# Turns given to the DMA queue by the slot that needs them, and the last keys' scores turned by DMA

## The chip, the cores and the metric

The kernel runs on one core of a Trainium2 chip. The metric is the device time of one execution in microseconds. Its engines are TensorE (PE in the profile; PEld is its weight load), VectorE (DVE), ScalarE (ACT), GpSimd (POOL) and SyncE (SP), which in this kernel issues every DMA, one after the other, from one list.

## What is computed

Two layers, one behind the other, for 8 batches of 3136 rows:

```python
scores = (1 / S) * z @ z.T           # z: 3136 x 64, S = 3136
attn   = maximum(scores, 0) ** 2
x      = u * (attn @ v)              # u, v: 3136 x 256
h      = xT @ U @ V                  # U: 3136 x 32, V: 32 x 3136, over the rows
u2     = x + hT
out    = u2 + maximum(u2 @ w_ch1, 0) @ w_ch2     # 256 -> 1024 -> 256
```

The matrix of scores is symmetric: the scores of keys J against queries g are the transpose of the scores of keys g against queries J. The kernel uses this, and so does the change.

## The kernel before, in words

**Tiles and groups.** The 3136 rows of a batch are 24 tiles of 128 and a rest of 64. Four tiles are a group of 512 rows, so a batch has six full groups (0 to 5) and a short one (6) with the last 64 rows. The program goes through 56 slots, one for each (batch, group), written (b, g) here; `t` counts them and `NG` is 7. In slot (b, g) the attention of group g of batch b is accumulated (`av_stream`, closed by `av_end`), and work of other stages lies between: scores for later slots, the low-rank part (`t1_all`, `u2_unit`) one batch behind, and the two channel products (`ch1_part`, `ch2_stream`) of the item one batch and one slot behind. The short slot (b, 6) has `av_small` in place of the attention stream.

**Scores and turns.** A block holds the squared scores of 512 keys J against 512 queries g, in bf16; there are 20 buffers for blocks. `score_pairs` makes half a block with two matmuls into one PSUM buffer of two banks, `rectify` (ScalarE, L335, or VectorE, L331) evicts it with the relu, and `square` (VectorE, L325) squares it. Only blocks with J >= g are made by matmuls, save for some of batch 0 that are made twice. The others are turned: a transposing DMA (`issue_turn`, L351) writes block (g, J) from block (J, g), 512 KB each, 15 in a batch (fewer in batch 0).

**The last 64 keys.** They meet the queries in two ways. For the last 64 queries, `score_small` makes one tile `attn_small` (128 keys, 25 tiles, 64 queries), which `av_small` reads in the short slot; before the change it is called in slot (b, 5). For the queries of groups 0 to 5, a job named "last", one for two groups, makes the scores of the last 64 keys against 2 x 512 queries: two matmuls side by side on the two halves of the rows, an eviction and a square into the tile `last_sb` (two buffers). `av_end` (L609) reads it as the last step of the attention of a group. `jobs_of` (L924) adds such a job for groups 0, 2 and 4 of each batch, and the jobs of group g are made in the slot before it; those of group 0 are spread over three slots of the batch before, and its last job falls into the short slot (for batch 1: into slot (1, 0)).

**The order of the work.** It is written out ahead of time by a planner that keeps a clock in units of 256 matmul columns (`clock`, `pe`) and an estimate of when ScalarE, VectorE and the DMA queue are free (`free_at`, `book`, `queued`). PSUM has four buffers (`take_ps` takes the one that it believes free first), one of them held by the attention stream. `emit` places the units of the other stages at given places between the attention's matmuls, later if it believes too few PSUM buffers free. `run_held` runs what is due, then issues turns: those whose source is squared wait in `ready_turns`, and one goes to SP whenever the estimate says that the queue is free and no `urgent` transpose is pending. It takes them in the order of the slot's group J, then the batch, then g. If the attention stream comes to a block that has not been issued, it issues the turn at that point (L521).

**Other DMAs on SP, in the same list.** Loads of u (L286), v (L234) and z (L211, L205), each batch's z transposed as a whole (`z_turn_dma`, L297, in slot (b, 2) for batch b + 1), the transpose of x into `u2T` for ch1 (`x_turn`, L634), and the stores of the result (L849). In slot (b, 0) the loads of z for the next batch come first, and u2T's transpose follows when `u2_unit` and its cast are done.

Of the kernel before, what the change touches and what calls it, by code (L numbers as in the profile page):

```python
# [18 lines left out]
def kernel(  # L19
# [79 lines left out]
    unturned = {}  # L99
    ready_turns = []  # L100
    urgent = []

    def book(eng, ready, cost):
        free_at[eng] = max(free_at[eng], ready) + cost
        return free_at[eng]

    def queued(kb, turned=False):

        book("sp", clock[0], kb * (17 / 256 if turned else 15 / 512))

    def hold(due, f):
        held.append((due, len(held), f))

    def run_held(now=None):
        now = clock[0] if now is None else now
        while True:
            ripe = [h for h in held if h[0] <= now]
            if not ripe:
                break
            h = min(ripe, key=lambda e: (e[0], e[1]))  # L120
            held.remove(h)
            h[2]()
        while ready_turns and free_at["sp"] <= now and not urgent:
            issue_turn(min(ready_turns, key=lambda e: (e[0], e[2], e[1])))

    def pe(cost):
        clock[0] += cost
# [218 lines left out]
    def issue_turn(e):  # L346
        ready_turns.remove(e)
        J, g, b = e
        src = blocks[b, g, J]
        blocks[b, J, g] = take_block()  # L350
        nc.sync.dma_start_transpose(  # L351
            out=blocks[b, J, g][1].rearrange("p j (q c) -> p (j q) c", c=P),
            in_=src[1].rearrange("p j c -> p (j c)"),
        )
        book("sp", clock[0], 34)
        if unturned.pop(src[0]):
            free_blocks.append(src[0])

    def score_pairs(jobs):

        made = []
        for b, g, job in jobs:
            zzT = zzTs[b]
            k, ps = take_ps()
            if job == "last":
                keys, cols = [NF, NF], [groups[g + jj][0] for jj in range(2)]
            else:
                J, h = job
                keys, cols = [J * GT + 2 * h + jj for jj in range(2)], [groups[g][0]] * 2
            pair(  # L370
                k,
                [
                    (
                        jj,
                        jj,
                        dict(
                            out=ps[:, jj, :],
                            lhsT=half(zzT, jj, keys[jj] * P, P),
                            rhs=half(zzT, jj, cols[jj], GW),
                            start=True,  # L380
                            stop=True,
                        ),
                    )
                    for jj in range(2)
                ],
                GW,
            )
            if job == "last":
                lasts[b, g // 2] = pool.tile([P, 2, GW], BF16, name="last_sb")
                made.append((lasts[b, g // 2], k, ps, None, None))  # L390
                continue
            if h == 0:
                blocks[b, g, J] = take_block()
            made.append(
                (
                    blocks[b, g, J][1][:, 2 * h : 2 * h + 2, :],
                    k,
                    ps,
                    (J, g, b) if h == 1 and J > g and not made_twice(b, J, g) else None,
                    (b, g, J),  # L400
                )
            )
        return made
# [19 lines left out]
        score_finish(score_pairs(jobs))  # L423


    def score_small(b, g):
        zzT = zzTs[b]
        g0, gw = groups[g]
        per = GW // gw
        att = pool.tile([P, NT, gw], BF16, name="attn_small")  # L430
        smalls[b] = att
        made = []
        npair = NF // 2
        for p0 in range(0, npair, per):
            n = min(per, npair - p0)
            pk, ps = take_ps()
            for k in range(n):
                pair(
                    pk,
                    [  # L440
                        (
                            jj,
                            jj,
                            dict(
                                out=ps[:, jj, k * gw : (k + 1) * gw],
                                lhsT=half(zzT, jj, (2 * (p0 + k) + jj) * P, P),
                                rhs=half(zzT, jj, g0, gw),
                                start=(k == 0),
                                stop=(k == n - 1 and (jj == 1 or p0 + n < npair)),
                            ),  # L450
                        )
                        for jj in range(2)
                    ],
                    gw,
                )
            made.append((p0, n, pk, ps))
        corner = ps[:, 0, n * gw : (n + 1) * gw]
        nc.tensor.matmul(
            out=corner,
            lhsT=half(zzT, 0, NF * P, P),  # L460
            rhs=half(zzT, 0, g0, gw),
            start=False,
            stop=True,
        )
        for p0, n, k, pp in made:
            dst = att[:, 2 * p0 : 2 * (p0 + n), :].rearrange("p (k j) c -> p j k c", j=2)
            src = pp[:, :, : n * gw].rearrange("p j (k c) -> p j k c", c=gw)
            for jj in range(2):
                nc.scalar.activation(out=dst[:, jj], in_=src[:, jj], func=AF.Relu, scale=scale)
                ps_free[k] = book("act", clock[0] + 3, 5)  # L470
        nc.scalar.activation(out=att[:TAIL, NF, :], in_=corner[:TAIL], func=AF.Relu, scale=scale)
        nc.vector.memset(att[TAIL:, NF, :], 0.0)
        ps_free[pk] = book("act", clock[0] + 3, 2.5)
        hold(ps_free[pk], lambda: square(att, 9))
# [87 lines left out]
    def av_small(b, g):  # L562
        k, ps = take_ps()
        rows = groups[g][1]
        xs[b, g] = pool.tile([P, GT, D], BF16, name="x_bf", bufs=8)
        for jt in range(NT):
            c = jt % 2
            for h in range(2):
                nc.tensor.matmul(  # L569
                    out=ps[c * hp : c * hp + rows, h, :D],  # L570
                    lhsT=smalls[b][h * hp : (h + 1) * hp, jt, :],
                    rhs=v_bfs[b][h * hp : (h + 1) * hp, jt, :],
                    start=(jt < 2),
                    stop=(jt >= NT - 2),
                    tile_position=(h * hp, c * hp),
                )
        pe(NT / 2 + 2)
        u1 = u_sbs[b, g]
        four_sums(k, ps, u1[:rows, 1:3, :])
        nc.vector.tensor_tensor(  # L580
            out=xs[b, g][:rows, 0, :], in0=u1[:rows, 1, :], in1=u1[:rows, 0, :], op=ALU.mult
        )
        book("dve", clock[0] + 3, 3)
# [24 lines left out]

    def av_end(b, g, box):  # L609

        last = lasts[b, g // 2]
        for a in range(2):
            pair(
                box["k"],
                crossed(
                    0,
                    a,
                    lambda h, q: dict(
                        out=four(box["ps"])[:, q, :],
                        lhsT=last[h, g % 2, q * P : (q + 1) * P],  # L620
                        rhs=v_bfs[b][h, NF, :],
                        start=False,
                        stop=(a == 1),
                    ),
                ),
                D,
            )
        av_out(b, g, box)
# [295 lines left out]
    def jobs_of(b, g):  # L924
        js = [J for J in range(NQ) if J >= g or made_twice(b, g, J)]
        j = [(b, g, (J, h)) for J in js for h in range(2)]
        if g % 2 == 0:
            j.append((b, g, "last"))
        return j

# [153 lines left out]
    for b in range(B):  # L1084
        for g in range(NQ):
# [7 lines left out]
                todo[t + 1] += new[12:] if b == 1 else []  # L1093
            elif b == 0 and g == 0:
                todo[0] += new[4:]
            else:
                todo[t] += new

# [3 lines left out]

    direct = (B - 1, 0)
    for t in range(n_items):
        att = items[t]
        u2i = items[t - NG] if t >= NG else None
        mix = items[t - NG - 1] if t > NG else None
# [26 lines left out]
                hold(clock[0] + 5 + 22 * i, lambda f=f: load(f))  # L1134
        if t <= NG:
            hold(clock[0] + 60, lambda t=t: load_u(*items[t + 1]))
        if b_next < B and g_now == 2:
            while spare:
                spare.pop(0)()
            z_turn_dma(b_next)  # L1140
# [14 lines left out]
        one = lambda h, way: lambda: ch1_part(*mix, h, way, box1)  # L1155
        hs = list(range(0, NH, 2)) if mix else []
        full = mix and mix[1] < NQ
        if av and g_now == NQ - 1:
            qm.append((55, 2, False, lambda: score_small(att[0], NQ)))
        if av and full:  # L1160

            last = nA - 9
# [111 lines left out]
```

## Time and profile before

| what | us |
|---|---|
| median of 3 runs (1003.33 to 1005.26) | 1004.55 |
| the profiled execution | 1002.76 |
| its span | 1001.0 |
| TensorE busy | 984.9 (98%) |
| VectorE busy | 655.9 (66%) |
| ScalarE busy | 520.3 (52%) |
| DMA queue, packets' share of 16 engines' span | 77.1% |

How to read it: times are microseconds from the start of the span; an engine is busy when one of its instructions runs. Matmuls overlap, so what one of them costs is seen from the start of one to the start of the next, not from its length. In a timeline, a row is a run of equal instructions: start, length until the last one ends, engine, line of the kernel, operation, output <- inputs with buffer numbers left out, shape, count, and in brackets the idle time before it with what ended it. Rows of one engine overlap by the length of the last instruction. SP's rows are the times in which it issues a DMA; the transfer lands later. L169 is a helper that issues all paired matmuls, so these are told apart by their tiles: `zzT` alone is scores, `v_bf,blk` attention, `u2T,w_bf` ch1, `w_bf,blk` ch2, `t_sb,V_bf` the u2 product, `v_bf,last_sb` av_end. Batch 0 differs from the others (loads of the weights, blocks made twice); from batch 1 on the program nearly repeats by batch.

### The profile page before, as it was taken

Reading aid. Unit: us, or ns where it says so; the run is one execution under the profiler, and the core shown is the slowest. Engines: PE = TensorE matmul, PEld = TensorE weight load, DVE = VectorE, ACT = ScalarE, POOL = GpSimd, SP = SyncE. Lnnn points to the kernel's source line nnn. Section 1 sums busy time; section 2 is a strip of 40 time slices with the busy share of each in tenths; the row PEclk is TensorE's granted clock in tenths of the full one; section 3 lists DMA queues with packets and bytes.
Section 4 is the critical chain, followed back from the end, with each engine's and each line's share of the span. In section 5 each row is a group of like instructions: output and inputs, shape, how many; then the busy total and the mean of one; then the engine's idle time right before and its main releaser. Section 6 shows DMA issues by size and latency. Waiting matters only on the chain.

```text
span 1001.0 us, 35345 instructions
## 1 busy us (share of the span) xinstructions
PE 984.9 (98%) x16179; PEld 820.1 (82%) x16179; DVE 655.9 (66%) x822; ACT 520.3 (52%) x597; POOL 16.6 (2%) x24
## 2 busy tenths in 40 slices
PE   6999999999999999999999999999999999999997
PEld 4898888877888788887888878888888877787776
DVE  6986856668566776666856677566775667653453
ACT  6896843457335473345643465435653356522453
POOL 4100000000000000000000000000000000000000
PEclk9999999999999999999999999999999999999999
DMA  8997898978886799877897789976889586863142
GB/s 260 197 252 177 188 182 182 196 164 190 168 205 137 177 174 183 191 129 183 157 217 166 141 179 176 198 170 139 182 186 194 142 170 143 154 126 89 45 104 95
DMA packets 337061, 167.84 MB, mean 168 GB/s; under 512 B 312336, under 2 KB 315408, under 8 KB 336912
## 3 DMA queue, kind: packets, MB, share of 16 engines
q1 hardware_dynamic: 336912, 165.59, 77.1%
q8 instruction: 126, 2.06, 0.9%
q14 instruction: 23, 0.19, 0.1%
HBM read 62.56 MB, written 25.69 MB: 88 GB/s over the span
## 4 chain that ended last, share of the span: by engine, by line
PE 94%; DVE 3%; ACT 2%; issue 0%; DMA 0%; POOLq 0%; ACTq 0%
PE ps L169 92%; DVE blk L325 1%; PE ps L569 1%; ACT blk L810 1%; PE ps L646 1%; DVE out_sb L719 1%; ACT blk L335 1%; PE ps L861 0%; DMA blk<-in_z_dram 0%; DVE blk L331 0%; DVE blk L847 0%; DVE blk L1065 0%; DVE x_bf L602 0%; PE ps L306 0%; ACT zzT L315 0%
## 5 line engine op out<-in xcount | busy, mean ns | idle before, releaser
L169 PEld LDWEIGHTS <-blk 64*128 64x128 bf16 x12288 | 647.6, 94 | 123.6 <-POOLq L159 8.7
L169 PE MATMUL ps<-v_bf,blk 64*128 64x256 bf16 x9216 | 620.4, 269 | 3.3 <-DVE blk L325 2.8
L335 ACT ACTIVATE blk<-ps 128x1024 bf16<-128x1024 f32 x334 | 333.1, 1027 | 330.3 <-PE ps L169 328.5
L325 DVE TENSOR_TENSOR blk<-blk 128x1024 bf16<-128x1024 bf16 x352 | 237.3, 700 | 34.1 <-ACT blk L335 33.3
L169 PE MATMUL ps<-u2T,w_bf 64*128 64x512 bf16 (+1 forms) x1792 | 240.7, 349 | 0.7
L807 DVE TENSOR_SCALAR blk<-ps 128x1024 bf16<-128x1024 f32 (+1 forms) x114 | 132.1, 1159 | 96.1 <-PE ps L169 95.2
L169 PE MATMUL ps<-w_bf,blk 64*128 64x256 bf16 x3072 | 194.1, 269 | 0.2
L169 PE MATMUL ps<-zzT 64*128 64x512 bf16 (+1 forms) x944 | 144.9, 341 | 2.3 <-ACT zzT L315 1.7
L810 ACT ACTIVATE blk<-ps 128x1024 bf16<-128x1024 f32 (+1 forms) x110 | 93.4, 859 | 82.7 <-PE ps L169 75.2
L169 PEld LDWEIGHTS <-w_bf 64*128 64x128 bf16 x1792 | 95.8, 94 | 27.4 <-POOLq L159 3.0
L602 DVE TENSOR_TENSOR x_bf<-ps,u_sb 128x1024 bf16<-128x1024 f32 x48 | 58.7, 1222 | 62.0 <-PE ps L169 61.9
L719 DVE TENSOR_TENSOR out_sb<-ps,x_bf 128x1024 f32<-128x1024 f32 (+1 forms) x49 | 54.2, 1107 | 51.1 <-PE ps L169 50.8
L847 DVE TENSOR_TENSOR out_sb<-ps,out_sb 128x1024 f32<-128x1024 f32 x42 | 51.3, 1222 | 18.3 <-PE ps L169 18.3
L169 PEld LDWEIGHTS <-zzT 64*128 64x128 bf16 x944 | 46.1, 95 | 8.4 <-issue 2.6
L335 ACT ACTIVATE last_sb<-ps 128x1024 bf16<-128x1024 f32 x23 | 23.6, 1024 | 28.4 <-PE ps L169 28.4
L169 PE MATMUL ps<-t_sb,V_bf 64*128 64x256 bf16 x200 | 21.1, 269 | 0.0
L331 DVE TENSOR_SCALAR blk<-ps 128x1024 bf16<-128x1024 f32 x14 | 17.1, 1224 | 5.6 <-PE ps L169 4.8
L191 DVE CAST v_bf<-stage 128x1024 bf16<-128x1024 f32 (+1 forms) x30 | 20.0, 670 | 0.0
L191 DVE CAST x_bf<-out_sb 128x1024 bf16<-128x1024 f32 x28 | 19.3, 690 | 0.5
L169 PE MATMUL ps<-v_bf,last_sb 64*128 64x256 bf16 x192 | 18.8, 269 | 0.0
L847 DVE TENSOR_TENSOR blk<-ps,blk 128x1024 f32<-128x1024 f32 x6 | 7.3, 1225 | 16.0 <-PE ps L169 15.9
L588 ACT COPY u_sb<-ps 64x512 f32<-64x512 f32 x8 | 4.7, 582 | 23.9 <-PE ps L569 23.9
(68 smaller groups left out, 255.7 us busy)
## 6 DMA issues: line engine op xcount, KB each, us to landing
u_sb<-in_u_dram SPq DMA_DIRECT2D x48, 512.0 KB, 5.1
stage<-in_v_dram SPq DMA_DIRECT2D x42, 512.0 KB, 6.0
out_dram<-out_sb SPq DMA_DIRECT2D x42, 512.0 KB, 3.1
stage<-in_z_dram SPq DMA_DIRECT2D x7, 512.0 KB, 5.4
blk<-in_v_dram SPq DMA_DIRECT2D x6, 512.0 KB, 6.2
out_dram<-blk SPq DMA_DIRECT2D x6, 512.0 KB, 2.6
blk<-in_moe_w_ch_dram SPq DMA_DIRECT2D x4, 512.0 KB, 4.9
stage<-in_z_dram SPq DMA_DIRECT2D x7, 256.0 KB, 5.7
```

The lines of the kernel that those rows point to most:

```text
L169: ins = nc.tensor.matmul(**args)
L191: nc.vector.tensor_copy(out=out, in_=in_)
L325: nc.vector.tensor_tensor(out=a, in0=a, in1=a, op=ALU.mult)
L331: nc.vector.tensor_scalar(out=dst, in0=src, scalar1=scale, scalar2=0.0, op0=ALU.mult, op1=ALU.max)
L335: nc.scalar.activation(out=dst, in_=src, func=AF.Relu, scale=scale)
L569: nc.tensor.matmul(out=ps[c * hp : c * hp + rows, h, :D], lhsT=smalls[b][h * hp : (h + 1) * hp, jt, :], rhs=v_bfs[b][h * hp : (h + 1) * hp ...
L602: nc.vector.tensor_tensor(out=xs[b, g][:rows, :n, :], in0=four(box["ps"])[:rows, :n, :], in1=u_sbs[b, g][:rows, :n, :], op=ALU.mult,)
L646: nc.tensor.matmul(out=pt[c * R : (c + 1) * R, 0, :D], lhsT=U_bf[:rows, it, :], rhs=xs[b, g][:rows, q, :], start=(it < NREP), stop=(it + N ...
L719: nc.vector.tensor_tensor(out=o[:rows, :n, :], in0=four(ps)[:rows, :n, :], in1=x, op=ALU.add)
L807: nc.vector.tensor_single_scalar(out=r, in_=ps[:, :, :gw], scalar=0.0, op=ALU.max)
L810: nc.scalar.activation(out=r, in_=ps[:, :, :gw], func=AF.Relu)
L847: nc.vector.tensor_tensor(out=o, in0=acc, in1=o, op=ALU.add)
```

## The change

**Turns.** They are now taken by `needed`: the slot that reads the block (batch times 7 plus J), then g. A turn goes to SP when the estimate of the queue is free, or up to 30 units ahead of that when it is needed in this slot or the next. The estimate counts less for each transfer: 30 in place of 34 for a turned block, 15/256 in place of 17/256 a KB for other transposes, 12/512 in place of 15/512 for plain ones.

**Last keys.** For batches 1 to 7 the "last" jobs are gone. At the start of slot (b, 0), `last_turn` gives SP one transpose of 24 tiles of `attn_small` (128 x 1536 bf16) into a tile `last_sb` of 128 x 12 x 128, behind the loads of that slot; `av_end` reads that tile. For this, `score_small` of batch b is called one batch earlier, in slot (b - 1, 5), and that of batch 0 in slot (0, 4). It makes the key tiles in the order 0, 2, 1, 3 of each four (`place_of`), so that the two halves of the rows of the turned tile hold the query tiles that `av_end` pairs; `av_small` reads them in that order too. Batch 0 keeps its three last jobs, which now use the first part of the same single buffer; those for groups 2 and 4 are made one slot later, in the slot that reads them.

```diff
@@ queued, run_held, issue_turn
+    slot = [0]
+    def needed(e):
+        J, g, b = e
+        return b * NG + J, g
...
-        book("sp", clock[0], kb * (17 / 256 if turned else 15 / 512))
+        book("sp", clock[0], kb * (15 / 256 if turned else 12 / 512))
...
-        while ready_turns and free_at["sp"] <= now and not urgent:
-            issue_turn(min(ready_turns, key=lambda e: (e[0], e[2], e[1])))
+        while ready_turns and not urgent:
+            e = min(ready_turns, key=needed)
+            if free_at["sp"] > now + (30 if needed(e)[0] <= slot[0] + 1 else 0):
+                break
+            issue_turn(e)
...
-        book("sp", clock[0], 34)
+        book("sp", clock[0], 30)
@@ score_pairs
-                lasts[b, g // 2] = pool.tile([P, 2, GW], BF16, name="last_sb")
+                flat = last_tile().rearrange("p n c -> p (n c)")
+                lasts[b, g // 2] = flat[:, : 2 * GW].rearrange("p (a c) -> p a c", c=GW)
@@ new, ahead of score_small
+    def place_of(jt):
+        if jt == NF:
+            return jt
+        return jt // GT * GT + (0, 2, 1, 3)[jt % GT]
+    def last_tile():
+        return pool.tile([P, NF // 2, P], BF16, name="last_sb", bufs=1)
+    def last_turn(b):
+        lasts[b] = last_tile()
+        nc.sync.dma_start_transpose(
+            out=lasts[b], in_=smalls[b][:, :NF, :].rearrange("p t c -> p (t c)")
+        )
+        book("sp", clock[0], 26)
@@ score_small
-                                lhsT=half(zzT, jj, (2 * (p0 + k) + jj) * P, P),
+                                lhsT=half(zzT, jj, place_of(2 * (p0 + k) + jj) * P, P),
@@ av_small
-                    lhsT=smalls[b][h * hp : (h + 1) * hp, jt, :],
+                    lhsT=smalls[b][h * hp : (h + 1) * hp, place_of(jt), :],
@@ av_end
-        last = lasts[b, g // 2]
+        def last(h, q):
+            if b:
+                return lasts[b][h, 2 * g + q % 2, :]
+            return lasts[b, g // 2][h, g % 2, q * P : (q + 1) * P]
...
-                        lhsT=last[h, g % 2, q * P : (q + 1) * P],
+                        lhsT=last(h, q),
@@ jobs_of
-        if g % 2 == 0:
+        if g % 2 == 0 and b == 0:
             j.append((b, g, "last"))
@@ the jobs of each slot
+            elif b == 0 and g and g % 2 == 0:
+                todo[t] += new[:-1]
+                todo[t + 1] += new[-1:]
@@ the loop over slots
+        slot[0] = t
...
+        if g_now == 0 and t:
+            last_turn(att[0])
...
-        if av and g_now == NQ - 1:
-            qm.append((55, 2, False, lambda: score_small(att[0], NQ)))
+        if av and t == NQ - 2:
+            qm.append((55, 2, False, lambda: score_small(0, NQ)))
+        if av and g_now == NQ - 1 and b_next < B:
+            qm.append((55, 2, False, lambda: score_small(b_next, NQ)))
```

## The prediction

> **What bounds the kernel now.** I read the busy shares first, then the chain of waits, then the groups by form, and at last the timelines of the few places where TensorE stops.
>
> The page, busy time and chain:
> ```profile
> span 1001.0 us, 35345 instructions
> ...
> PE 984.9 (98%) x16179; PEld 820.1 (82%) x16179; DVE 655.9 (66%) x822; ACT 520.3 (52%) x597; POOL 16.6 (2%) x24
> ...
> PE 94%; DVE 3%; ACT 2%; issue 0%; DMA 0%; POOLq 0%; ACTq 0%
> ```
> TensorE is busy from end to end, and the granted clock is 1.0 throughout. The waits name no DMA on TensorE at all: no turn ever came late. So only two things shorten the time: fewer matmul columns, and less of the small idle time in front of matmuls. The groups that the change thins out, by form:
> ```profile
> L169 PE MATMUL ps<-zzT 64*128 64x512 bf16 x752 | 140.7, 380 | 2.3 <-ACT zzT L315 1.7
> ...
> L335 ACT ACTIVATE last_sb<-ps 128x1024 bf16<-128x1024 f32 x23 | 23.6, 1024 | 28.4 <-PE ps L169 28.4
> ...
> L325 DVE TENSOR_TENSOR last_sb<-last_sb 128x1024 bf16<-128x1024 bf16 x24 | 16.4, 683 | 0.2 <-ACT last_sb L335 0.2
> ```
> The "last" job is made 24 times: two 512-column matmuls, one eviction of 1024 ns, one square of 683 ns. The mean of 380 ns is the length of one matmul, and they overlap; what one costs TensorE is read from starts. TensorE's timeline in the short slot (group 6) of batch 2:
> ```profile
> 331.42 0.60 PE L169 MATMUL ps<-u2T,w_bf 64*128 64x512 bf16 x4
> 331.85 0.39 PE L169 MATMUL ps<-zzT 64*128 64x512 bf16 x2
> 332.07 1.90 PE L169 MATMUL ps<-u2T,w_bf 64*128 64x512 bf16 x16
> 333.79 0.39 PE L169 MATMUL ps<-zzT 64*128 64x512 bf16 x2
> 334.27 1.47 PE L169 MATMUL ps<-u2T,w_bf 64*128 64x512 bf16 x12
> ```
> Eight pairs run from 332.07 to 333.79: 0.215 us a pair. The pair at 333.79 is a "last" job, and the next starts 0.48 us later, so 0.27 us of that is a stall. ScalarE in the same stretch says for what:
> ```profile
> 333.20 1.02 ACT L810 ACTIVATE blk<-ps 128x1024 bf16<-128x1024 f32 x1
> 334.22 1.02 ACT L335 ACTIVATE last_sb<-ps 128x1024 bf16<-128x1024 f32 x1
> ```
> The matmul at 334.27 needs the PSUM buffer that the eviction of 333.20 gives back at 334.22. The "last" job took the buffer before it (given back at 333.30).
>
> The second stop is in slot (b, 1); TensorE, then VectorE:
> ```profile
> 364.18 0.60 PE L169 MATMUL ps<-v_bf,blk 64*128 64x256 bf16 x8
> 364.61 0.38 PE L169 MATMUL ps<-zzT 64*128 64x512 bf16 x2
> 364.83 0.71 PE L169 MATMUL ps<-v_bf,blk 64*128 64x256 bf16 x10
> 365.66 0.39 PE L169 MATMUL ps<-zzT 64*128 64x512 bf16 x2
> ```
> ```profile
> 364.38 1.23 DVE L719 TENSOR_TENSOR out_sb<-ps,x_bf 128x1024 f32<-128x1024 f32 x1
> ```
> Five pairs from 364.83 need 5 x 0.109 = 0.55 us (0.109 from 8 matmuls in 0.43), yet the score pair starts 0.83 us later, when L719 has emptied its buffer: a stall of 0.28 us. Both stops come back every 121.92 us, the period of a batch in the chain (332.28, 454.20, 576.11).
>
> **The change, part by part.**
>
> *Last jobs.* Batches 1 to 7 lose three each: 21 pairs x 0.2157 = 4.53 us of TensorE, with no cover since TensorE is the bound. The 21 evictions (21 x 1.02 us of ScalarE) and 21 squares lie beside it. av_end keeps its matmuls and reads another tile.
>
> *Short slot, batches 1 to 6.* The last job left the short slot, so the matmul after it takes the buffer that is free at 333.30, while TensorE gets there at 333.79: the 0.27 us goes. 6 x 0.27 = 1.6 us. What is late next is the last relu before ch2 (ended 337.01, cost 0.10 us by a gap before 337.06); it may eat some, so 1.0 to 2.2, and I take 1.6.
>
> *Slot (b, 1).* With one job fewer, the list of places spreads: in the built program the score after u2 now stands behind 6 attention pairs and no other score, and the buffer that it takes is not the one which L719 empties. The stop shows in batches 2 to 6, at 243.75, 365.66, 487.58, 609.49 and 731.41. Between none and all, 0 to 5 x 0.28 = 1.4; I take two thirds, 0.9, since evictions near it shift too.
>
> *Slot (1, 0).* At 109.43 TensorE waits for the cast of v_bf, the end of a DVE queue without a gap from 101.40, in which the square of last_sb (0.69 us at 102.01) goes. The stall there is 0.64 us. Bounds 0 and 0.64; I take 0.3, as that queue is also reordered.
>
> *score_small one batch earlier.* The same 8 calls; 0.35 us of TensorE each (the 12 pairs run from 321.57 to 321.92), moved from group 5 of batch 7 to group 4 of batch 0. Evictions and square (16 x 0.61, 16 x 0.42 and 8 x 0.99 us in all) go along, onto engines at 52% and 66%. Zero, between -0.3 and +0.5.
>
> *The new transpose, 7 times.* 128 x 1536 bf16 = 393 KB on the only queue. It goes to SP behind the loads of z at the start of slot (b, 0). Its place in SP's list:
> ```profile
> 346.03 1.55 SPq L205 DMA_DIRECT2D stage<-in_v_dram  x2
> 350.30 2.21 SPq L634 DMA_TRANSPOSE u2T<-x_bf  x1
> ```
> SP is free from 347.58 to 350.30. A block's turn of 512 KB holds SP 2.83 us (median of line 351), u2T's of 256 KB 1.25, so this one some 2.0: it fits the gap. The DMA engines, by windows (the last two numbers are share and GB/s):
> ```profile
> 343.50:348.50 5.00, 5.00 (x102) 4.23 (x98) 4.48 (x8) 3.03 (x6) 0.00 (x0) 1.00 1.00 338
> 349.50:351.50 2.00, 2.00 (x44) 1.78 (x37) 1.66 (x5) 1.24 (x3) 0.00 (x0) 1.00 0.10 25
> 354.00:356.00 2.00, 2.00 (x38) 1.60 (x34) 1.93 (x5) 0.69 (x1) 0.00 (x0) 1.00 1.15 214
> ```
> They stand idle from 349.5 to 351.5, and turns move 214 GB/s, so 393 KB take 1.84 us: about the size of that hole. Landing by the rows (3.3 us for u2T, 5.2 for a block) is some 4.2 us after issue, 351.8; av_end reads at 356.02. Behind it waits u2T's turn, issued 350.30, landed 354.7, first read 356.68: margin 2.0 us. If the transpose is pushed out of the hole by up to 1.84 us, u2T still lands by 356.5. Bounds 0 and 7 x 1.0; I take 0.5 in all. The Trainium skill, page "Advanced Engine Details and Errata", section "X-Bar Transpose (TRN2)", says that transposing DMAs run as fast as plain ones; here they run at 214 GB/s against 338 for loads, so the measurement decides. By the page it would be 1.16 us instead of 1.84, more margin, and the sum the same.
>
> *Order and figures of the turns.* Turned blocks stand, in the built programs, at least 22 us of matmuls ahead of their first reader before and 27 us after, against 5 us to land: neither gain nor loss from their order. What moves is queue order. In slot (b, 2) one more block's turn (2.83 us on SP) now stands between the turn of zzT and that of u2T; u2T landed at 390.05 there and is read at 395.93, 5.9 us of margin. The blocks that ScalarE writes into have, in the built program, been read for the last time 3.7 us or more before. Zero, between -0.2 and +2.
>
> *Batch 0.* Its three last tiles now share one buffer, and two of the jobs move one slot on; ScalarE's write waits for the av_end before, while TensorE goes on. Zero.
>
> Sum: -4.53 - 1.6 - 0.9 - 0.3 + 0.5 = -6.8 us. The profiled execution took 1002.76 us (span 1001.0 and 1.76 around it), which becomes 996.0; it lies 1.8 below the median of the runs, 1004.55, which becomes 997.7.
>
> **The rivals.**
>
> *Columns alone.* The stops move instead of going (a later eviction or the cast is late). Then -4.5 and up to +1.5 of new waits: 1000.0 to 1001.5. Against it: the chain is empty elsewhere.
>
> *Slower: u2T late at the start of slot (b, 1).* The new transpose misses the hole, and SP's 2.0 us and the engines' 1.84 both delay u2T: 3.84 less the margin of 2.0 is a stall of 1.84 in each of 7 batches, +12.9; net +6.1, 1010.6. It decides from 2.0 + 6.8 / 7 = 3.0 us of delay. For it: in batch 4 the margin was 1.15 us (landed 477.44, read 478.60). Against it: idle DMA engines just there. The Trainium skill, "DMA: Bandwidth & Descriptors", section "Queues, rings and completion order", has each engine consume its ring in order, which is the mechanism of this rival; no row here shows a u2T packet behind another transpose's in that slot.
>
> *Nothing gained: the saving goes into half-late u2T turns.* A delay near 3.0 us in each batch gives about 1004.5.
>
> **How the numbers follow.** Forecast 0.62, columns alone 0.22, nothing gained 0.07, slower 0.09. 0.2% (2 us) is about what a measurement here can tell. All of the gains taken whole, -4.53 - 2.2 - 1.4 - 0.64 = -8.8, give 995.8, and runs spread by 1.2 below the median: low 994.5. Columns alone with new waits reach 1001.5, with spread 1002.2: high. Outside lie the two last cases and a little of the first. Faster 0.84, same 0.07, slower 0.09.
>
> **What would show it.** Right: 42 matmuls and 21 evictions fewer; no gap before the ch1 matmuls of the short slot; the period 121.92 down to about 120.9; the wait for L719 gone or small; the new transpose landed before 353; no DMA in TensorE's waits. Wrong: TensorE waiting for u2T or last_sb at the start of slot (b, 1), or new waits on evictions where scores moved.

## The result, and the profile after

The changed kernel takes 998.55 us (median of 6 runs, 997.68 to 999.23) against 1004.36 (6 runs, 1003.33 to 1005.26): a ratio of 0.9946, with a 95% interval of 0.9936 to 0.9956. The forecast was 997.7 us and a gain of 6.8; the gain is 5.8. The profiled execution took 997.68 us, its span is 995.9.

The page of the changed kernel, busy times and chain (line numbers have moved: L178 was L169, L344 L335, L334 L325, L750 L719, L198 L189, L596 L569):
```profile
span 995.9 us, 35255 instructions
...
PE 979.2 (98%) x16137; PEld 781.5 (78%) x16137; DVE 635.6 (64%) x793; ACT 506.4 (51%) x584; POOL 16.8 (2%) x24
...
PE 97%; DVE 1%; ACT 1%; DMA 1%; issue 0%; POOL 0%; SPq 0%; POOLq 0%
```
42 matmuls are gone, and TensorE's share of the chain went from 94% to 97%: VectorE and ScalarE are hardly in it any more. The groups by form:
```profile
L178 PE MATMUL ps<-zzT 64*128 64x512 bf16 x710 | 131.2, 381 | 1.7 <-ACT zzT L324 1.7
...
L334 DVE TENSOR_TENSOR last_sb<-last_sb 128x1024 bf16<-128x1024 bf16 x3 | 2.1, 687 | 0.2 <-ACT last_sb L344 0.2
L344 ACT ACTIVATE last_sb<-ps 128x1024 bf16<-128x1024 f32 x2 | 2.0, 1021 | 0.6 <-PE ps L178 0.6
```
752 became 710, and three squares are left, those of batch 0. The chain in order of time shows the length of a batch by the 50 matmuls of the short slot, first before and then after:
```profile
337.67 1.54 PE ps L569 x50
...
459.59 1.54 PE ps L569 x50
```
```profile
338.10 1.54 PE ps L596 x50
...
458.83 1.54 PE ps L596 x50
```
A batch takes 120.73 us, where it took 121.92. The 1.19 us are three pairs (0.65), the stop in the short slot (0.27) and the one in slot (b, 1) (0.28), to the rounding. TensorE in the short slot of batch 2, timeline:
```profile
332.30 0.62 PE L178 MATMUL ps<-u2T,w_bf 64*128 64x512 bf16 x4
332.73 0.40 PE L178 MATMUL ps<-zzT 64*128 64x512 bf16 x2
332.95 3.21 PE L178 MATMUL ps<-u2T,w_bf 64*128 64x512 bf16 x28
335.97 0.27 PE L178 MATMUL ps<-w_bf,blk 64*128 64x256 bf16 x1
```
The 14 pairs of ch1 run from 332.95 to 335.97 in one row: 0.216 each, no stop. In slot (b, 1):
```profile
364.38 0.38 PE L178 MATMUL ps<-t_sb,V_bf 64*128 64x256 bf16 x4
364.60 0.82 PE L178 MATMUL ps<-v_bf,blk 64*128 64x256 bf16 x12
365.26 0.38 PE L178 MATMUL ps<-zzT 64*128 64x512 bf16 x2
365.47 0.59 PE L178 MATMUL ps<-u2T,w_bf 64*128 64x512 bf16 x4
```
Six attention pairs take 0.66 us and the score pair follows at once.

One wait grew. TensorE and VectorE in slot (1, 0) before:
```profile
108.04 0.93 PE L169 MATMUL ps<-v_bf,blk 64*128 64x256 bf16 x14
109.43 0.83 PE L169 MATMUL ps<-v_bf,blk 64*128 64x256 bf16 x12 [0.46 <-DVE v_bf L191]
```
```profile
108.69 0.68 DVE L191 CAST v_bf<-stage 128x1024 bf16<-128x1024 f32 x1
```
TensorE and ScalarE there after:
```profile
108.81 1.36 PE L178 MATMUL ps<-v_bf,blk 64*128 64x256 bf16 x22
111.94 1.05 PE L178 MATMUL ps<-v_bf,blk 64*128 64x256 bf16 x16 [1.77 <-ACT v_bf L198]
```
```profile
106.18 2.92 ACT L344 ACTIVATE blk<-ps 128x1024 bf16<-128x1024 f32 x3 [0.74 <-PE ps L178]
108.99 1.05 ACT L198 CAST w_bf<-blk 128x1024 bf16<-128x1024 f32 x1
109.92 1.04 ACT L344 ACTIVATE blk<-ps 128x1024 bf16<-128x1024 f32 x1
110.84 1.05 ACT L198 CAST v_bf<-stage 128x1024 bf16<-128x1024 f32 x1
```
The cast of v_bf, which VectorE did before, is now on ScalarE behind another cast and an eviction. From start to start, TensorE comes to 111.94 1.95 us later than the matmuls before it need; before the change it lost 0.64 us there, at 109.43.

The new transpose in SP's timeline at the start of slot (2, 0):
```profile
225.70 1.24 SPq L214 DMA_DIRECT2D stage<-in_v_dram  x2
227.04 2.25 SPq L448 DMA_TRANSPOSE last_sb<-attn_small  x1
229.96 1.64 SPq L665 DMA_TRANSPOSE u2T<-x_bf  x1
```
It sits in SP's gap, and SP is done with it (229.29) before u2T's turn goes out. No DMA appears in TensorE's waits.

Not all of the difference of the two traces belongs to the change. Up to 30 us the lists of all engines are the same, and yet one and the same matmul of slot (0, 2) starts here:
```profile
32.24 0.28 PE L169 MATMUL ps<-v_bf,blk 64*128 64x256 bf16 x2 [0.94 <-DVE blk L325]
```
```profile
33.27 0.28 PE L178 MATMUL ps<-v_bf,blk 64*128 64x256 bf16 x2 [0.93 <-DVE blk L334]
```
before in the first fence, after in the second. Over the profiles of this study, that matmul starts at 32.0 to 33.8 us. So the difference of the spans, 5.1 us, holds 1.0 us of a slower beginning, and without it is 6.1. The last section compares all runs from this matmul on.

### The profile page after: what moved, and what is told of

Its sections match the earlier page's. It is cut to its first block, busy times and chain, and to the rows that moved or that the text cites. A ratio compares the mean times of both kernels' runs of the same rounds, so it can differ in the third digit from the quotient of the medians.

```text
span 995.9 us, 35255 instructions
## 1 busy us (share of the span) xinstructions
PE 979.2 (98%) x16137; PEld 781.5 (78%) x16137; DVE 635.6 (64%) x793; ACT 506.4 (51%) x584; POOL 16.8 (2%) x24
## 4 chain that ended last, share of the span: by engine, by line
PE 97%; DVE 1%; ACT 1%; DMA 1%; issue 0%; POOL 0%; SPq 0%; POOLq 0%
PE ps L178 94%; PE ps L596 1%; PE ps L677 1%; DVE blk L334 1%; DMA blk<-in_v_dram 1%; PE ps L892 0%; ACT blk L344 0%; ACT blk L841 0%; DVE blk L340 0%; POOL z_bf L229 0%; DVE blk L878 0%; DVE x_bf L629 0%; POOL v_bf L249 0%; PE ps L315 0%; ACT v_bf L198 0%
## 5 line engine op out<-in xcount | busy, mean ns | idle before, releaser
L178 PEld LDWEIGHTS <-blk 64*128 64x128 bf16 x12288 | 616.1, 94 | 154.3 <-POOLq L168 8.8
L178 PE MATMUL ps<-v_bf,blk 64*128 64x256 bf16 x9216 | 614.0, 270 | 3.2 <-ACT v_bf L198 1.8
L344 ACT ACTIVATE blk<-ps 128x1024 bf16<-128x1024 f32 x334 | 334.3, 1027 | 363.3 <-PE ps L178 361.5
L334 DVE TENSOR_TENSOR blk<-blk 128x1024 bf16<-128x1024 bf16 x352 | 237.4, 699 | 33.6 <-ACT blk L344 33.1
L178 PE MATMUL ps<-u2T,w_bf 64*128 64x512 bf16 (+1 forms) x1792 | 237.2, 349 | 0.2
L178 PE MATMUL ps<-w_bf,blk 64*128 64x256 bf16 x3072 | 193.8, 269 | 0.2
L838 DVE TENSOR_SCALAR blk<-ps 128x1024 bf16<-128x1024 f32 (+1 forms) x111 | 128.4, 1156 | 96.5 <-PE ps L178 95.6
L178 PE MATMUL ps<-zzT 64*128 64x512 bf16 (+1 forms) x902 | 135.3, 341 | 1.7 <-ACT zzT L324 1.7
L178 PEld LDWEIGHTS <-w_bf 64*128 64x128 bf16 x1792 | 91.9, 94 | 28.9 <-POOLq L168 4.1
L750 DVE TENSOR_TENSOR out_sb<-ps,x_bf 128x1024 f32<-128x1024 f32 (+1 forms) x49 | 54.2, 1106 | 50.3 <-PE ps L178 49.9
L178 PEld LDWEIGHTS <-zzT 64*128 64x128 bf16 x902 | 41.8, 95 | 7.4 <-ACT zzT L324 2.2
L178 PE MATMUL ps<-t_sb,V_bf 64*128 64x256 bf16 x200 | 20.8, 269 | 0.0
L200 DVE CAST v_bf<-stage 128x1024 bf16<-128x1024 f32 x28 | 19.1, 683 | 0.0
L178 PE MATMUL ps<-v_bf,last_sb 64*128 64x256 bf16 x192 | 18.6, 269 | 0.0
L198 ACT CAST v_bf<-stage 128x1024 bf16<-128x1024 f32 (+1 forms) x20 | 17.1, 856 | 0.0
L617 DVE TENSOR_TENSOR u_sb<-ps,u_sb 64x512 f32<-64x512 f32 x8 | 5.5, 683 | 17.1 <-ACT u_sb L615 17.1
```

Source lines behind the costliest of these rows:

```text
L178: ins = nc.tensor.matmul(**args)
L198: nc.scalar.copy(out=out, in_=in_)
L200: nc.vector.tensor_copy(out=out, in_=in_)
L334: nc.vector.tensor_tensor(out=a, in0=a, in1=a, op=ALU.mult)
L344: nc.scalar.activation(out=dst, in_=src, func=AF.Relu, scale=scale)
L750: nc.vector.tensor_tensor(out=o[:rows, :n, :], in0=four(ps)[:rows, :n, :], in1=x, op=ALU.add)
```

## The experiments

Each ran beside the kernel before on the same chip, four on one chip and four on another; ratios are against that kernel.

**The turn rule alone.** The kernel before with `needed`, the gate and the smaller figures, without anything of the last keys:

```diff
-            issue_turn(min(ready_turns, key=lambda e: (e[0], e[2], e[1])))
+            e = min(ready_turns, key=needed)
+            if free_at["sp"] > now + (30 if needed(e)[0] <= slot[0] + 1 else 0):
+                break
+            issue_turn(e)
...
+ (and 30, 15 / 256, 12 / 512 for 34, 17 / 256, 15 / 512)
```

> The kernel before with the new rule and figures for the turns alone; the last jobs stay. TensorE, ScalarE and VectorE have the same lists as before; SP's list alone changes. Theory A (the gain is 21 score pairs and two kinds of PSUM stops, the turns' order does nothing, since every turned block is issued 27 us or more ahead of its reader): 1004.4, within 1 us, TensorE's waits unchanged, the stops of 0.28 and 0.27 us still there in each batch. Theory B (part of the 5.8 us comes from the turn rule, which lets blocks or u2T land earlier): 1 to 3 us faster. Theory C (the rule costs, and hides more gain of the last jobs): 1 to 3 us slower, a TensorE wait on a DMA.

Measured: 1003.36 us against 1003.49, ratio 0.9997 (0.9987 to 1.0007). Theory A: all stops of 0.27 and 0.28 us are where they were, and no DMA is waited for. On the kernel before, the rule is worth nothing that can be measured.

**The last keys alone.** The changed kernel with the old rule and the old figures. The lists of TensorE, VectorE and ScalarE are those of the changed kernel.

```diff
-            e = min(ready_turns, key=needed)
-            if free_at["sp"] > now + (30 if needed(e)[0] <= slot[0] + 1 else 0):
-                break
-            issue_turn(e)
+            issue_turn(min(ready_turns, key=lambda e: (e[0], e[2], e[1])))
...
- (and 34, 17 / 256, 15 / 512 again)
```

> The changed kernel with the old rule and the old figures for the turns. Theory A: the same as the changed kernel, 998.5, within 1 us, and the wait of 2 us in slot (1, 0) still there, since VectorE and ScalarE have the same lists. Theory B: 1 to 3 us of the gain is lost, 999.5 to 1001.5. Theory C: 1 to 3 us faster than the changed kernel.

Measured: 1004.99 us, ratio 1.0019 (1.0009 to 1.0028). No theory had this: the whole gain is gone, and the run is a little slower than the kernel before. TensorE's timeline and then SP's say where:
```profile
203.97 0.28 PE L175 MATMUL ps<-v_bf,blk 64*128 64x256 bf16 x2
210.25 1.25 PE L175 MATMUL ps<-v_bf,blk 64*128 64x256 bf16 x10 [6.00 <-DMA blk<-blk]
```
```profile
197.72 6.11 SPq L357 DMA_TRANSPOSE blk<-blk  x2
203.93 1.88 SPq L662 DMA_TRANSPOSE u2T<-x_bf  x1
205.86 2.06 SPq L357 DMA_TRANSPOSE blk<-blk  x1
```
The last turned block that slot (1, 5) reads is issued at 205.86, when TensorE has already come to it, and lands 4.3 us later. In the built program this turn stands directly ahead of its reader; every other turn stands at least 13 us of matmuls ahead. Three turns of batch 2, which are read 46 to 73 us after their place, were taken ahead of it: the old order compares the group first and the batch second, so groups 1, 2 and 3 of batch 2 pass group 5 of batch 1. On the kernel before, the same order never let a turn fall under 12.8 us. With the new transpose booked on the estimate (26 units), the queue counts as free later, the turn waits longer, and the attention stream itself has to call for it (L521 in the kernel before). Built without that booking, the program issues this turn 11.8 us of matmuls ahead of its reader; that program was not run, so the booking's part is read from the programs and not shown by a time. (The two expectations that follow put the turn 1.9 us ahead of its reader and 18 us or more in the other programs; counted by start-to-start costs, the distances are these smaller ones, and the turns ahead of it are three and not two.) The late turn comes once in 1000 us and stops TensorE for 6.2 us from start to start.

The stop costs more than its length, because the granted clock falls in it. Two windows of the same trace, one within the stop and one right behind it (of the last three numbers, the first is the granted clock):
```profile
207.00:210.00 3.00, 0.00 (x0) 0.00 (x0) 0.00 (x0) 0.00 (x0) 0.00 (x0) 0.50 0.98 183
210.20:213.50 3.30, 3.25 (x30) 2.22 (x32) 0.00 (x0) 1.02 (x1) 0.00 (x0) 0.50 0.00 0
```
The clock is 1.00 from 204 to 206.5, 0.50 from 207 to 213.5, and 1.00 again from 214. Behind the stop, a pair of 256 columns takes 0.21 us in place of 0.109. This adds 1.6 us, so that the one late turn costs 7.8 us in all, more than the change gains. In the changed kernel, the stop of 1.95 us in slot (1, 0) leaves the clock at 1.00.

**Which half of the rule is needed.** The same, with the new order and the old figures and gate; then with the new figures and the old order and gate:

```diff
-            issue_turn(min(ready_turns, key=lambda e: (e[0], e[2], e[1])))
+            issue_turn(min(ready_turns, key=needed))
```
```diff
-        book("sp", clock[0], kb * (17 / 256 if turned else 15 / 512))
+        book("sp", clock[0], kb * (15 / 256 if turned else 12 / 512))
...
-        book("sp", clock[0], 34)
+        book("sp", clock[0], 30)
```

> The changed kernel with the old figures and the old gate, but turns taken by the slot that needs them. In the run with the old rule, TensorE waited 6.0 us once, in slot (1, 5), for a turned block that stood 1.9 us of matmuls ahead of its reader, behind two turns for batch 2. Theory A (the old order puts batch 2's group 1 ahead of batch 1's group 5; only that turn is late): with the new order the smallest distance in the built program is 18 us, so no wait on a DMA, and the time of the changed kernel, 998.5, within 1. Rival (the figures of the estimate cause it, they hold turns back): the wait stays, 1004 to 1005.

> The changed kernel with the old order and the old gate of the turns, but the new, smaller figures. Theory A (late is the one turn that the estimate holds back until the reader comes; with smaller figures the queue counts as free early enough, the smallest distance in the built program is 27 us): no wait on a DMA, 998.5 within 1, so that either half of the rule alone is enough. Rival (the order is what matters): a wait of several us on a turned block, 1002 to 1005.

Measured: 996.46 us, ratio 0.9932 (0.9919 to 0.9945) with the order; 997.41 us, 0.9939 (0.9925 to 0.9954) with the figures. Neither waits for a turned block; both intervals overlap the changed kernel's. Either half is enough, so neither "the order" nor "the figures" is needed by itself: both lead away from the one late turn. The gate alone was not run. The rival of the first run is out, and so is that of the second.

**The wait in slot (1, 0).** The changed kernel with the casts due earlier:

```diff
-            hold(clock[0] + (90 if g_now == NQ else 15 if t > NG else 45) + 12 * i, f)
+            hold(clock[0] + (60 if t == NQ else 90 if g_now == NQ else 15 if t > NG else 45) + 12 * i, f)
```

> The changed kernel with the casts of slot (1, 0) made due 60 units after the start of the short slot (0, 6), in place of 90; TensorE's list is the same. Theory A (the 1.95 us stop at 111.94 is TensorE waiting for a cast that is put into ScalarE's list too late): the stop is gone, 998.55 - 1.9 = 996.6. Rival (the stop is only the place where lateness of that slot shows, by scores or by loads that land late): it comes back within the slot at another wait, 998 to 998.6.

Measured: 995.2 us, ratio 0.9916 (0.9903 to 0.9929), below the interval of the changed kernel. Its TensorE and ScalarE in that slot:
```profile
108.92 2.24 PE L178 MATMUL ps<-v_bf,blk 64*128 64x256 bf16 x38
```
```profile
105.42 2.00 ACT L198 CAST w_bf<-blk 128x1024 bf16<-128x1024 f32 x2
107.31 1.04 ACT L344 ACTIVATE blk<-ps 128x1024 bf16<-128x1024 f32 x1
108.22 1.06 ACT L198 CAST v_bf<-stage 128x1024 bf16<-128x1024 f32 x1
```
The cast starts at 108.22 in place of 110.84, on the same engine, and TensorE runs through the place in one row. The edit also moved one cast of w_bf from VectorE to ScalarE. The stop is gone, and nothing took its place: theory A. The trace accounts for 1.9 us; the ratios differ by 3 us, of which the rest is within the intervals. This kernel has the lowest median of the study.

**The stop in the short slot, with no column saved.** The kernel before, with group 0's last job moved into slot (b, 0) for batches 2 to 7:

```diff
-                todo[t] += new[y:12] if b == 1 else new[y:]
-                todo[t + 1] += new[12:] if b == 1 else []
+                todo[t] += new[y:12]
+                todo[t + 1] += new[12:]
```

> The kernel before with all its 24 last jobs, but the one of group 0 moved from the short slot into slot (b, 0), for batches 2 to 7. No column is saved. Theory A (the stop of 0.27 us in the short slot is a wait for the PSUM buffer that the last job pushed one eviction on): the stop is gone in 6 short slots, 1004.4 - 1.6 = 1002.8, if the job finds room in slot (b, 0). Rival (the stop belongs to the slot, whose ch2 waits for its last relu anyway): the wait moves to ch2, 1004.0 to 1004.8, with a gap of 0.3 us before ch2's matmuls in place of 0.10.

Measured: 1004.67 us, ratio 1.0014 (1.0005 to 1.0024). TensorE in the short slot, and then in slot (b, 0):
```profile
211.09 3.19 PE L169 MATMUL ps<-u2T,w_bf 64*128 64x512 bf16 x28
```
```profile
229.31 0.51 PE L169 MATMUL ps<-v_bf,blk 64*128 64x256 bf16 x6
230.00 0.39 PE L169 MATMUL ps<-zzT 64*128 64x512 bf16 x2 [0.18 <-ACT blk L335]
```
The stop left the short slot with the job, as A has it, and no new wait appeared before ch2. But the job now meets full PSUM buffers in slot (b, 0): 0.36 us from start to start, in each of six batches, waiting for an eviction. So the 0.27 us were the price of that job's place, and in the other place that was tried it pays a little more. Where it is dropped, the whole of it is saved.

**How much room the DMA queue has.** The new transpose issued twice, the first time into a free block that nobody reads:

```diff
+        k, spare_block = take_block()
+        nc.sync.dma_start_transpose(
+            out=spare_block.rearrange("p a (n c) -> p (a n) c", c=P)[:, : NF // 2, :],
+            in_=smalls[b][:, :NF, :].rearrange("p t c -> p (t c)")
+        )
+        free_blocks.append(k)
         lasts[b] = last_tile()
```

> The changed kernel with the new transpose issued twice, first into a free block that nobody reads, then into its own tile: 7 x 393 KB more in the queue, in front of u2T's turn of slot (b, 0). Theory A (the new transpose lies in a hole of the DMA queue that holds one, and u2T has 0.8 to 3.1 us of margin left behind it): SP is held 2.0 us and the engines 1.84 us longer, u2T comes late in three to five of seven batches by 0.3 to 1.2 us, 999.5 to 1002.5, with TensorE waiting for u2T at the start of slot (b, 1). Rival (the DMA queue has room for much more): 998.5 within 0.7. Rival (it is at its end already): each batch late by 1.84 us, 1010 or more.

Measured: 1000.2 us, ratio 0.9970 (0.9958 to 0.9982). TensorE at the start of slot (2, 1), and SP before it:
```profile
235.88 0.60 PE L178 MATMUL ps<-v_bf,blk 64*128 64x256 bf16 x8
237.09 0.60 PE L178 MATMUL ps<-u2T,w_bf 64*128 64x512 bf16 x4 [0.61 <-DMA u2T<-x_bf]
```
```profile
226.92 2.07 SPq L448 DMA_TRANSPOSE blk<-attn_small  x1
229.09 2.90 SPq L454 DMA_TRANSPOSE last_sb<-attn_small  x1
232.08 1.26 SPq L671 DMA_TRANSPOSE u2T<-x_bf  x1
```
u2T's turn goes out at 232.08 in place of 229.96, and TensorE waits for it in four batches: 0.79, 0.46, 0.45 and 0.28 us from start to start, 2.0 in all. Theory A, inside its numbers. The single runs lie between 997.4 and 1003.8 us, wider than those of any other kernel here, so one trace gives the waits of one execution only. This is the price of what lies just beyond the change: the queue has room for one such transpose there, and not for a second one without a cost.

**No transpose from batch 2 on.** Batches 2 to 7 read batch 1's tile, which leaves out the transposes; the last 64 keys' share of groups 0 to 5 in those batches is then batch 1's:

```diff
+        if b > 1:
+            lasts[b] = lasts[1]
+            return
         lasts[b] = last_tile()
```

> The changed kernel with the new transpose issued for batch 1 alone; batches 2 to 7 read batch 1's tile, so the share of the last 64 keys is wrong for groups 0 to 5 of those batches, and nothing else. TensorE, ScalarE and VectorE have the same lists. Theory A (the transposes are wholly covered): the same as the changed kernel, 998.5 within 0.7. Rival (they cost some 0.5 us in all, or more, by contention in the DMA queue): 0.5 to 2 us faster, 996.5 to 998.

Measured: 996.82 us, ratio 0.9941 (0.9929 to 0.9952), against 0.9946 (0.9936 to 0.9956) with the transposes. The stops are the same in both traces, one by one. By the ratios, up to about 2 us could hide in the intervals. The traces are closer: from the matmul of slot (0, 2) to the last row of TensorE they take 953.75 and 953.74 us, so six of the transposes cost TensorE nothing.

## Why the prediction was right, and where not

*Last jobs, -4.53 us.* Right: 42 matmuls and 21 evictions fewer, and 0.216 us a pair in the period of a batch.

*Short slot, -1.6 us.* Right, 0.27 in each of six; the relu before ch2 still stops TensorE by about 0.08 us, as before.

*Slot (b, 1), -0.9 us.* Mis-sized by the caution: all five stops are gone, so it is -1.4.

*Slot (1, 0), -0.3 us.* Wrong in sign: +1.31. The prediction took one square out of VectorE's queue and held the cast to stay on it. The planner gives a cast to whichever of ScalarE and VectorE it believes free first. Before, it believed VectorE free first at this cast (962.7 against 967.0 on its clock); after, with the last job's eviction gone from ScalarE and its square from VectorE, it believed ScalarE free first (963.2 against 967.6). There a cast of w_bf and an eviction lay ahead. The cause that was named (a cast too late) was right, as the run with early casts shows; that the thinned queue would be the one to use was not. It alone is 1.6 us against the forecast; two other terms came out 0.5 us better each. So it is in part luck that the sum came out close: an error of 1.6 us stands against two of 0.5 the other way.

*score_small one batch earlier, 0.* Right within what the trace tells: no new stop in slots (0, 4) and (0, 5).

*The new transpose, +0.5 us.* It costs nothing that can be measured. The hole, SP's free time and the margins were read rightly, the landing was taken too short: SP is held 2.0 us (median of the seven; 1.5 to 2.7), it lands 3.7 to 7.2 us after issue (4.2 was forecast, the median is 5.6), and u2T's margin at the start of slot (b, 1) fell from 4.7 us to 1.5 in batch 1 and by up to 1.2 in the others, to 0.84 at the least. The doubled transpose shows that this margin is real. One sign of being right was not met: in the slot whose rows the prediction shows, the transpose landed at 354.75 and not before 353, 1.7 us ahead of its reader at 356.45.

*Order and figures of the turns, 0.* The number was right on the kernel before (0.9997). The distances were read too large: counted in the built programs from a turn's place to the first matmul that reads its block, with 0.109 us for a pair of 256 columns and 0.216 for one of 512, the smallest is 12.8 us before and 20.1 after, not 22 and 27 (and 13.0 and 20.1 in the two runs with half of the rule). Against some 5 us to land, the conclusion holds all the same. As a statement on the change it was incomplete: the distances were read in the kernel before and in the whole changed kernel, not in the changed kernel without the rule. There one turn stands directly ahead of its reader, and costs 7.8. So the rule adds nothing to the gain and yet carries all of it; that the term of zero did not spoil the sum is owed to the rule's being part of the change. The prediction's rivals had u2T as the DMA that comes late; the one that came late without the rule was a block's turn.

Sum by the runs: -4.53 - 1.6 - 1.4 + 1.3 = -6.2 us. From the matmul of slot (0, 2) on, the traces differ by 6.17 us; the slower beginning makes 5.1 of it by the spans, and the medians say 5.8. The rival of columns alone (1000.0 to 1001.5) is out, since the stops went; the rivals of a late u2T are what the doubled transpose makes true in part.

## What to carry to other kernels

When a kernel is bound by one engine and an estimate plans its queues, count the effect of each part of a change with the other parts taken away: a part that does nothing by itself can be what keeps another from a late transfer, and the distance in program order between a transfer and its reader shows it before any run. A small job costs more than its columns where it takes a buffer that the next one waits for; here, moved, it paid in its new place, and only dropped it saved the whole. Where a planner picks the engine by an estimate, an instruction less on one engine can move another one to a worse place, so read the new list of each engine and not only the old one minus the removed lines.

## What the runs showed that was not expected

The beginning of the program varies by itself: with the same lists on all engines, the first matmul after the stop in slot (0, 2) started at 32.0 to 33.8 us over ten profiles; the cause stays open. A comparison of two single traces by their spans carries that 1.8 us; the period of a batch does not. Nor does the time from that matmul to the last row of TensorE (64 matmuls of ch2), which every trace has:

| run | slot (0, 2) | last row | between, us |
|---|---|---|---|
| before | 32.24 | 992.16 | 959.92 |
| the turn rule alone | 32.04 | 991.94 | 959.90 |
| the changed kernel | 33.27 | 987.02 | 953.75 |
| old figures, new order | 32.25 | 985.99 | 953.74 |
| new figures, old order | 33.67 | 987.42 | 953.75 |
| no transpose from batch 2 on | 32.45 | 986.19 | 953.74 |
| the new transpose twice | 33.19 | 989.36 | 956.17 |
| early casts | 33.38 | 985.22 | 951.84 |
| the last keys alone | 33.84 | 995.39 | 961.55 |
| a last job moved, on the kernel before | 33.17 | 993.71 | 960.54 |

Four programs agree to 0.01 us here, while their medians lie between 996.5 and 998.6. Read so, the change gains 6.17 us, the early casts 1.91 more, the second transpose costs 2.42, and the late turn 7.80.

A turn that is late once costs more than the whole change gains: 7.8 us for one block. Of the stop's 6.2 us, 4.3 are its landing and most of the rest u2T's turn, which SP issued ahead of it while TensorE stood; the other 1.6 us are the matmuls at half clock behind the stop.
